# The last 768 tokens' output product by seven half-width products instead of eight

## The chip, the cores and the metric

One core of one Trainium2 chip runs the whole program. The metric is the time of one execution on the device in microseconds (us); the time before is the median of three runs.

## The reference, cut to what matters

```
attention: q, k, v [8 batches, 8 heads, 576, 64]; k and v are averaged over groups of 8 positions (72 left)
  scores = q @ k_pooled.T / 8;  softmax over the 72;  x = attn @ v_pooled     -> x [4608 tokens, 512]
h   = x @ w_in                          # w_in  [512, 2048]
g   = h * clip(h + 3, 0, 6) / 6
out = g @ w_out                         # w_out [2048, 512], out [4608, 512], float32
```

## The kernel before, in words

The 4608 tokens are cut into 12 blocks: 512, 256, 384, 384 and then eight of 384. The first four are plain ("x @ w_in, gate, g @ w_out", lines L822 and L853). The last eight are taken in pairs of 768 tokens, here called supers 0 to 3 (`super_block`). All operands of large products are split into a high and a low part of a 32-bit format that TensorE multiplies at full rate, so each product is three matmuls: high by high, high by low, low by high.

A super has two phases. The **hidden phase** (matmuls at L1065) forms h by a 2x2 split (two token halves of 384, two halves of the 512 inputs, two feature rows of a pair `i`) with seven products instead of eight; its combinations of w_in were formed once, during blocks 2 and 3, and stored in DRAM tiles `wd`. The PSUM sums (`psx`) are copied by ScalarE (`keep`, L1044) or added by VectorE (`plus`, L1039) and gated (L1032, L1033) into `g`. There are 56 products of 6 matmuls with 384 columns each. The **output phase** (matmuls at L1111) is plain: for each of the 16 feature groups f, `split_g` makes the high part (ScalarE, L1050) and the low part (VectorE, L1051) of 128x768 elements of g, and each of six token tiles of 128 takes three matmuls of 512 columns. In super 3 the last token tile is done in two halves of 256 columns, in its own banks, so that its copies start earlier. That makes 288 matmuls in supers 0 to 2 and 240 of 512 plus 96 of 256 columns in super 3.

The weights of both phases stream from DRAM in chunks of 512 KB, one for two products of the hidden phase and one for each f of the output phase. They go through eight SBUF buffers, four in each of two pools (`wsFalse`, `wsTrue`), and `chunk` asks for each one seven ahead. All of these loads, the loads of q, k and v, and the stores of out stand in SyncE's queue (SP), in one order: a transfer that waits holds back those behind it.

The attention of the next two blocks runs within a super: 45% of its steps are spread over the hidden phase and the rest over the output phase (`Paced`). Pooling of k and v is VectorE's (L250, L371), the softmax is ScalarE's and VectorE's with GpSimd dividing (L488). At the end of the output phase `x_ops` forms the seven combinations of x for the next super. Supers 0 to 2 carry such work; super 3 has none, as no block follows.

Within each engine the framework's scheduler sets the order, from its own estimate of times; for the program's first stretch (blocks 0 and 1) a written table (`ORDER`) sets it. The table is the same in both kernels.

Of the kernel before, what the change touches and what calls it, by code (L numbers as in the profile page):

```python
# [17 lines left out]
P = 128  # L18
# [20 lines left out]
RAW = {1: (0, 0), 2: (0, 1), 4: (1, 1)}  # L39
CHUNK, NSTREAM, NFIRST, NC, NREL = 2, 8, 4, 6, 3  # L40
TAIL = 5
# [48 lines left out]
def attention_moe_kernel(  # L90
# [267 lines left out]

    vsum = {}

    def prep_v(b, p):


        if p == 0:
            if b not in W:
                place_v(b)
            sums = ring("vsum")[:, : (NPAIR + NG) * D]
            vsum[b] = sums.rearrange("p (c d) -> p c d", d=D)
        n = P if p < NPAIR else 3 * REM
        vs, st = vsum[b], vraw.pop((b, p))  # L370
        nc.vector.tensor_reduce(  # L371
            out=vs[:n, p], in_=st[:n, : POOL * D].rearrange("p (o d) -> p d o", o=POOL), axis=AX.X, op=ALU.add
        )
        after_mark()
        if p == NPAIR - 1:
            place_heads(b, vs[:, :NPAIR])
        elif p == NPAIR + NG - 1:
            place_rest(b, vs[:, NPAIR:])

    def place_heads(b, vs):  # L380
        whi, wlo, _ = W[b]
        for h in range(2):
            rows, cols = slice(h * D, (h + 1) * D), slice(h * D, (h + 1) * D)
            hi = whi[rows, :, cols]
            nc.scalar.mul(hi, vs[rows], 1.0 / POOL)
# [251 lines left out]
    def side_steps(b):  # L637

        ks = [lambda p=p: load_k(b, p) for p in range(NPAIR)]
        ks += [lambda p=p: prep_k(b, p) for p in range(NPAIR)]  # L640
        vs = []
        n = NPAIR + NG
        for p in range(n + 2):
            if p < n:
                vs.append(lambda p=p: load_v(b, p) if p < NPAIR else load_vr(b, p - NPAIR))
            if p >= 2:
                vs.append(lambda p=p: prep_v(b, p - 2))
        return ks, vs
# [254 lines left out]
    w_dram = [tc.dram_tile([P, CHUNK, 2, 2 * P], F32, name=f"wd{n}") for n in range(len(N1) // CHUNK)]  # L903
    w2_dram = [tc.dram_tile([P, 2, DM], F32, name=f"w2d{f}") for f in range(NF)]

# [27 lines left out]
    def plain_of(i, n):  # L933
        if n < 2:
            for o, (r, q) in list(RAW.items())[2 * n : 2 * n + 2]:
                store(dram_of(i, o), pair_of(i)[r][:, :, q])
        else:
            f = 2 * i + n - 2
            store(w2_dram[f], w_of[f, 1].bitcast(F32))

    late = []
    chunks = [w for _ in supers for w in (*w_dram, *w2_dram)]
    loaded = {}

    def chunk(n, ahead=NSTREAM - 1):

        while (m := len(loaded)) <= n + ahead and m < len(chunks):
            if m % NSTREAM >= NFIRST and len(late) < 2:
                break
            side = m % NSTREAM >= NFIRST  # L950
# [3 lines left out]
            t, src = loaded[m].bitcast(F32), chunks[m]  # L954
            if len(src.shape) == 4:
                src = src.rearrange("p k m c -> p (k m c)")
            else:
                src = src.rearrange("p m c -> p (m c)")
            nc.sync.dma_start(t, src)
            mark()  # L960
        return loaded[n]

    PER = len(w_dram) + len(w2_dram)

    def next_w(n, m):
        t = chunk(n * PER + m // CHUNK)
        return t.rearrange("p (k m c) -> p k m c", k=CHUNK, m=2)[:, m % CHUNK]

    def next_w2(n, f):
        return chunk(n * PER + len(w_dram) + f).rearrange("p (m c) -> p m c", m=2)  # L970

    x_op = {}

    def x_ops(j):
# [3 lines left out]
        def split(o, src):  # L978
            def make(c):
                if c == 0:  # L980
                    x_op[o] = late[0].tile([P, 2, 2, HALF], F32R, name=f"x{o}")
                t, x = x_op[o][:, :, c], src()[:, c]
                nc.scalar.copy(t[:, 0], x)
                nc.vector.tensor_tensor(out=t[:, 1], in0=x, in1=t[:, 0].bitcast(F32), op=ALU.subtract)  # L984

            return [lambda c=c: make(c) for c in range(2)]

# [31 lines left out]
    def super_block(n, j, first_att, second_att):  # L1019

        ops = dict(x_op)
        att_banks[:] = ["a0", "a1", "o3"]
        g_of, chain, parts = {}, {}, {}
        paced = Paced(first_att, len(N1) - 2)
# [17 lines left out]
        def keep(ps):  # L1042
            c = late[1].tile([P, HALF], F32, name="c", bufs=NC)
            nc.scalar.copy(c, ps)  # L1044
            return c

        def split_g(f):
            g = g_of[f // 2][:, f % 2 :: 2]
            hi, lo = (late[1].tile([P, 2, HALF], F32R, name=m, bufs=3) for m in ("ghi2", "glo2"))
            nc.scalar.copy(hi, g)  # L1050
            nc.vector.tensor_tensor(out=lo, in0=g, in1=hi.bitcast(F32), op=ALU.subtract)  # L1051
            mark()
            parts[f] = [t.rearrange("p h t -> p (h t)") for t in (hi, lo)]

        for m, (i, o) in enumerate(N1):
            if o == 1:
                g_of[i] = late[1].tile([P, 4, HALF], F32, name=f"g{i}")
                chain[i] = [bank(["h0", "h1", "o0"], i), bank(["o1"], i), bank(["o2"], i), {}]
# [25 lines left out]
        paced.upto(len(paced.steps))  # L1084

        NT2 = 2 * HALF // P
        rest = x_ops(j + 2) if j + 2 < len(BLOCKS) else []
        paced = Paced(second_att, NT2 * (NF - TAIL))
        split_g(0)
        att_banks[:] = ["a0", "a1"]  # L1090
        banks = ["o0", "h0", "o2", "o1", "h1", "o3"]
        sums = {}
        for f in range(NF):
            if f + 1 < NF:
                split_g(f + 1)
            w = next_w2(n, f)
            for t in range(NT2):
                if f < NF - TAIL:
                    paced.slot()
                elif rest:  # L1100
                    rest.pop(0)()
                hi, lo = (x[:, t * P : (t + 1) * P] for x in parts[f])
                products = (hi, 0), (hi, 1), (lo, 0)
                end = f == NF - 1
                if f == 0:
                    sums[t] = [(slice(0, DM), bank(banks, t, DM))]
                    if n == len(supers) - 1 and t == NT2 - 1:
                        sums[t] = [(slice(0, 256), sums[t][0][1][:, :256]), (slice(256, 512), bank(["a0"], 0, 256))]
                for cols, pos in sums[t]:
                    for k, (l, r) in enumerate(products):  # L1110
                        nc.tensor.matmul(pos, l, w[:, r, cols], start=f == 0 and k == 0, stop=end and k == 2)  # L1111
# [4 lines left out]
                tag, size = ("ro", DM) if t >= 4 else (("ghi2", "glo2")[t % 2], 2 * HALF)  # L1116
                o = late[1].tile([P, size], F32, name="o", tag=tag, bufs=3)[:, :DM]
                at = starts[j] + t * P
                for q, (cols, pos) in enumerate(sums[t]):
                    (nc.vector.tensor_copy if (t + q) % 2 else nc.scalar.copy)(o[:, cols], pos)  # L1120
                    nc.sync.dma_start(out[at : at + P, cols], o[:, cols])
            if f == NF - TAIL - 1:
                paced.upto(len(paced.steps))
        assert not rest

# [281 lines left out]
```

## Time and profile before

| what | value |
|---|---|
| median of 3 runs | 905.71 us (905.52 to 905.98) |
| the profiled execution | 905.32 us, of which the span of instructions is 903.5 us |
| TensorE busy | 884.1 us of 903.5 (98%) |
| VectorE, ScalarE busy | 571.4 us (63%), 513.6 us (57%) |
| DMA | 172.63 MB, mean 191 GB/s |
| granted TensorE clock | 1.00 throughout |

A row of the chain of waits gives the start, the duration and what ran there without a break; a row of the table by stages gives each engine's busy time in a stretch of the span. Busy time of TensorE counts a matmul from its start until its result is modelled to be out, and successive ones overlap: the pace of matmuls is read from their starts, not from their mean durations.

### The profile page before, as it was taken

The numbers are of one execution on the slowest core, as the hardware profiler recorded it, in microseconds if no ns is written. First come the engines' busy times: TensorE is split into PE (matmuls) and PEld (weight loads), VectorE is DVE, ScalarE is ACT, GpSimd is POOL, SyncE is SP. The second block draws the span as 40 slices with busy tenths as digits, with TensorE's granted clock in tenths as the row PEclk, the third lists the DMA queues.
The fourth block names the chain that finished last, engine by engine and source line by source line (L and its number), as shares of the span: only waits on it lengthen the run. The fifth ranks groups of instructions, "written<-read, shape, count | busy, mean of one in ns | idle before, by whom it ended". The sixth has DMA issues, their size and how long they took to land.

```text
span 903.5 us, 14091 instructions
## 1 busy us (share of the span) xinstructions
PE 884.1 (98%) x4760; PEld 796.8 (88%) x4760; DVE 571.4 (63%) x1183; ACT 513.6 (57%) x1473; POOL 86.2 (10%) x168
## 2 busy tenths in 40 slices
PE   7999999999999998999999999999999999999998
PEld 6788888998999987998888999888999888999887
DVE  6999855578876884875735856666677345554221
ACT  5998666656566654765535855454766344444121
POOL 4100002100202010201100100110100110000000
PEclk9999999999999999999999999999999999999999
DMA  9970207984415236977535786744877433767321
GB/s 297 392 278 0 94 1 241 398 293 136 111 52 177 59 129 216 375 251 236 163 104 191 242 281 203 238 154 153 271 249 258 140 117 116 266 231 269 120 70 70
DMA packets 93527, 172.63 MB, mean 191 GB/s; under 512 B 12048, under 2 KB 50704, under 8 KB 93456
## 3 DMA queue, kind: packets, MB, share of 16 engines
q1 hardware_dynamic: 93312, 171.74, 56.9%
q8 instruction: 38, 0.62, 0.3%
q14 instruction: 33, 0.27, 0.1%
q10 hardware_dynamic: 144, 0.00, 0.0%
HBM read 139.20 MB, written 32.51 MB: 190 GB/s over the span
## 4 chain that ended last, share of the span: by engine, by line
PE 83%; DVE 8%; DMA 4%; ACT 2%; SPq 1%; issue 1%; DVEq 0%; ACTq 0%
PE psx L1111 29%; PE psx L1065 25%; PE psh L822 10%; PE pso L853 10%; PE psa L452 3%; PE psa L628 3%; DMA wd<-wq 2%; DMA stage<-q_l 2%; PE psa L558 1%; SPq L928 1%; DVE wq L919 1%; DVE wq L924 1%; DVE wq L926 1%; ACT e L460 1%; DVE x L984 1%
## 5 line engine op out<-in xcount | busy, mean ns | idle before, releaser
L822 PE MATMUL psh<-xhi,w 128*128 128x384 f32 (+2 forms) x520 | 145.4, 339 | 1.1 <-DVE g L834 1.0
L1065 PE MATMUL psx<-x,wsFalse 128*128 128x384 f32 x672 | 130.7, 339 | 2.0 <-ACT o L858 1.0
L1065 PE MATMUL psx<-x,wsTrue 128*128 128x384 f32 x672 | 127.9, 339 | 3.8 <-DVE g L1033 2.6
L1051 DVE TENSOR_TENSOR glo<-g,ghi 128x768 fp32r<-128x768 f32 x64 | 63.5, 993 | 103.9 <-ACT ghi L1050 100.4
L1111 PE MATMUL psx<-wsFalse,ghi 128*128 128x512 f32 (+1 forms) x400 | 123.0, 388 | 0.0
L1111 PE MATMUL psx<-wsTrue,ghi 128*128 128x512 f32 (+1 forms) x400 | 122.7, 386 | 0.0
L853 PE MATMUL pso<-w,ghi 128*128 128x512 f32 x384 | 121.3, 400 | 0.0
L1065 PEld LDWEIGHTS psx<-x,wsTrue 128*128 128x128 f32 x672 | 116.8, 188 | 4.7 <-DVE g L1033 2.9
L1065 PEld LDWEIGHTS psx<-x,wsFalse 128*128 128x128 f32 x672 | 117.2, 188 | 2.9 <-ACT o L858 1.4
L1050 ACT CAST ghi<-g 128x768 fp32r<-128x768 f32 x64 | 53.4, 835 | 95.1 <-PE psx L1111 90.5
L822 PEld LDWEIGHTS psh<-xhi,w 128*128 128x128 f32 x520 | 93.3, 188 | 8.9 <-DVE g L834 1.8
L460 ACT ACTIVATE e<-psa,mx 128x72 f32<-128x72 f32 x256 | 78.3, 322 | 32.4 <-DVE mx L456 31.2
L1039 DVE TENSOR_TENSOR g<-psx,c 128x384 f32<-128x384 f32 x96 | 53.0, 555 | 59.2 <-ACT c L1044 33.3
L488 POOL TENSOR_TENSOR a<-e,sm 128x256 f32<-128x256 f32 x60 | 39.7, 662 | 517.1 <-DVE sm L477 443.0
L822 PE MATMUL psh<-xlo,w 128*128 128x384 f32 (+2 forms) x260 | 86.8, 335 | 0.0
L1111 PEld LDWEIGHTS psx<-wsFalse,ghi 128*128 128x128 f32 x400 | 73.6, 188 | 15.0
L1111 PEld LDWEIGHTS psx<-wsTrue,ghi 128*128 128x128 f32 x400 | 73.4, 188 | 13.4
L853 PEld LDWEIGHTS pso<-w,ghi 128*128 128x128 f32 x384 | 69.1, 188 | 10.2
L1111 PE MATMUL psx<-wsFalse,glo 128*128 128x512 f32 (+1 forms) x200 | 77.6, 388 | 0.0
L1111 PE MATMUL psx<-wsTrue,glo 128*128 128x512 f32 (+1 forms) x200 | 76.6, 383 | 0.0
L853 PE MATMUL pso<-w,glo 128*128 128x512 f32 x192 | 74.0, 399 | 0.0
L1032 ACT ACTIVATE r<-g,small 128x384 f32<-128x384 f32 x96 | 54.7, 612 | 25.5 <-DVE g L1039 21.0
(126 smaller groups left out, 1435.4 us busy)
## 6 DMA issues: line engine op xcount, KB each, us to landing
wsFalse<-wd SPq DMA_DIRECT2D x56, 512.0 KB, 4.5
wsTrue<-wd SPq DMA_DIRECT2D x56, 512.0 KB, 5.0
wsTrue<-w2d SPq DMA_DIRECT2D x32, 512.0 KB, 4.0
wsFalse<-w2d SPq DMA_DIRECT2D x32, 512.0 KB, 3.5
out<-o SPq DMA_DIRECT2D x35, 256.0 KB, 2.7
raw<-w_in_l SPq DMA_DIRECT2D x16, 512.0 KB, 8.5
raw<-w_out_l SPq DMA_DIRECT2D x16, 512.0 KB, 9.3
w2d<-w SPq DMA_DIRECT2D x16, 512.0 KB, 5.4
```

What stands on the lines that cost most here:

```text
L452: nc.tensor.matmul(to, qt[:, p, :], kbds[b % 2][:, p, :], start=r == 0, stop=r == last)
L460: nc.scalar.activation(self.e[:, h], self.ps[:, h], AF.Exp, bias=self.mx[:, h : h + 1], accum_out=self.sm[:, h : h + 1])
L488: engine.tensor_tensor(out=self.a[:, : 4 * D].rearrange("p (h s) -> p h s", h=4), in0=e[:, :, :D], in1=sm[:, :, None].broadcast_to([P, 4, D]),
L628: nc.tensor.matmul(ps, l, r, start=n == 0, stop=n == len(mms) - 1)
L822: nc.tensor.matmul(self.ps, l[f][:, c, :], r[:, c, :], start=c == 0 and i == 0, stop=c == NCC - 1 and i == 2)
L853: nc.tensor.matmul(pos, l, r, start=f == 0 and i == 0, stop=f == NF - 1 and i == 2)
L1032: nc.scalar.activation(r, src, AF.Relu, bias=half_low, scale=GSCALE / (6.0 * WSCALE))
L1039: nc.vector.tensor_tensor(out=g_of[i][:, k], in0=ps, in1=kept, op=ALU.add)
L1050: nc.scalar.copy(hi, g)
L1051: nc.vector.tensor_tensor(out=lo, in0=g, in1=hi.bitcast(F32), op=ALU.subtract)
L1065: nc.tensor.matmul(ps, w[:, l, c * P : (c + 1) * P], t[:, r, c], start=o in (1, 2, 5) and c == 0 and k == 0, stop=c == 1 and k == 2, skip_ ...
L1111: nc.tensor.matmul(pos, l, w[:, r, cols], start=f == 0 and k == 0, stop=end and k == 2)
```

## The change

**Output phase of super 3.** `out_seven` takes the place of the plain phase there. g is split by token half (384) and by feature parity, w_out by parity and by halves of its 512 columns. Seven kinds of products, in the order 1, 2, 4, 5, 6, 7, 3 (`KINDS`), each over four groups `m` of features: 28 steps, each of 3 token tiles x 2 feature rows x 3 matmuls of 256 columns. That is 504 matmuls of 256 columns. Kinds accumulate on each other's PSUM banks where the scheme allows (1, 6 and 7 on `X`; 5 and 3 on `Y`); ScalarE copies the sums of kinds 1, 4, 5 and 6 to SBUF (`to_sbuf`), VectorE adds the other part (`result`) and the store follows. VectorE also forms the combinations of g in place (`mix`), four for each m.

**The blocks of w_out for it.** Kinds 1, 2 and 3 read the stored w_out (`w2d`) in pieces; the other four need combinations. `combine` forms them in the output phases of supers 0 to 2 (three, three and two times), from the chunks that stream by for those phases: six additions and a subtraction on VectorE, one copy on ScalarE, and two stores of 512 KB into new DRAM tiles `w2t`.

**Values.** A pair of value tiles is loaded as two half-pieces and pooled by three wide additions, in place of two strided reductions (L371).

**Smaller things.** Seven stream buffers for eight; tiles for gates, kept sums and split parts in pairs; the combinations of x whole instead of in halves; 50% of the attention steps in the hidden phase instead of 45%; w_out is stored in column halves, so that the plain output phase reads its 512 columns in two pieces of 256.

```diff
-CHUNK, NSTREAM, NFIRST, NC, NREL = 2, 8, 4, 6, 3
+CHUNK, NSTREAM, NFIRST, NC, NREL = 2, 7, 4, 3, 2
+KINDS = (1, 2, 4, 5, 6, 7, 3)
+PLACED = {6: 0, 5: 1, 4: 2, 7: 3}
+RAW2 = {1: (0, 0), 2: (1, 0), 3: (1, 1)}
+SEVEN = (3,)
+MAKE = ((0, 1, 2), (3, 4, 5), (6, 7), ())
+CUTS = (0.5, 0.5, 0.5, 0)
...
     def prep_v(b, p):
-        nc.vector.tensor_reduce(
-            out=vs[:n, p], in_=st[:n, : POOL * D].rearrange("p (o d) -> p d o", o=POOL), axis=AX.X, op=ALU.add
-        )
+        x, y = (vraw.pop((b, p + i))[:n, : POOL * D].rearrange("p (c n) -> p c n", c=2) for i in range(2))
+        for w, a, c in ((4 * D, x, y), (2 * D, x, x[:, :, 2 * D :]), (D, x, x[:, :, D:])):
+            nc.vector.tensor_tensor(out=x[:, :, :w], in0=a[:, :, :w], in1=c[:, :, :w], op=ALU.add)
...
+    def combine(n, i):
+        hi, q = (
+            late[1].tile([P, 2 * DM], F32, name=x, tag="ro", bufs=NREL).rearrange("p (a c) -> p a c", a=4)
+            for x in ("th", "tq")
+        )
+        for r in range(2):
+            w = next_w2(n, 2 * i + r).bitcast(F32)
+            nc.vector.tensor_tensor(out=q[:, 2 * r : 2 * r + 2], in0=w[:, :, 0], in1=w[:, :, 1], op=ALU.add)
+        for to, a, b, how in ((3, 3, 1, ALU.subtract), (1, 1, 0, ALU.subtract), (0, 0, 3, ALU.add), (2, 2, 0, ALU.subtract)):
+            nc.vector.tensor_tensor(out=q[:, to], in0=q[:, a], in1=q[:, b], op=how)
+        nc.scalar.copy(hi.bitcast(F32R), q)
+        nc.vector.tensor_tensor(out=q.bitcast(F32R), in0=q, in1=hi, op=ALU.subtract)
+        for m, x in enumerate((hi, q)):
+            nc.sync.dma_start(w2t_dram[i // 2][:, :, i % 2, m], x)
...
+    def out_plain(n, j, bank, parts, split_g, split_f, pairs, att, rest, last_h):
...
+            if f % 2 == 0 and f // 2 in MAKE[n]:
+                combine(n, f // 2)
...
-                        nc.tensor.matmul(pos, l, w[:, r, cols], start=f == 0 and k == 0, stop=end and k == 2)
+                        to = pos.rearrange("p (q c) -> p q c", c=DM // 2)
+                        nc.tensor.matmul(to, l, w[:, qs, r], start=f == 0 and k == 0, stop=end and k == 2)
...
+    def out_seven(n, j, bank, parts, split_g, split_f, pairs, att, rest, last_h):
+        todo = [(o, m) for o in KINDS for m in range(NM)]
+        sets = {"X": ["o2", "o1"], "Z": ["o0", "o3"], "V": ["h1", "h0"], "Y": ["o0", "o3"]}
+        on = {2: "Z", 1: "X", 4: "V", 5: "Y", 6: "X", 7: "X", 3: "Y"}
...
+        for x, (o, m) in enumerate(todo):
+            upto(x + 2)
+            w, t = next_w2(n, x), parts[o, m]
+            for i in range(NT2):
+                to = ps[name][i // 2][:, i % 2 * W2 : (i % 2 + 1) * W2]
+                for k in range(2):
+                    for y, (l, r) in enumerate(((0, 0), (0, 1), (1, 0))):
+                        nc.tensor.matmul(
+                            to,
+                            t[:, l, k, i * P : (i + 1) * P],
+                            w[:, k, r],
...
+                        )
+            if m < NM - 1:
+                continue
+            if o in (1, 4, 5, 6):
+                to_sbuf(o)
+            if o == 2:
+                result(1, 0, 0, "Z")
+            elif o == 7:
+                result(5, 1, 1, "X")
+                result(4, 1, 0, "X")
+            elif o == 3:
+                result(6, 0, 1, "Y")
```

**How instructions move.** Three places follow. In a row stand the line, the operation, what it writes and reads, its size and how often it is repeated; numbers in names tell tiles of one kind apart.

VectorE, at the turn from the hidden to the output phase of super 3 (`g` are the gated sums, `glo` and `part` the low parts for the output phase), before:

```order
L1039 TENSOR_TENSOR g_9012<-psx,c 128x384 x2
L1033 SCALAR_TENSOR_TENSOR g_9012<-r,g_9012 128x384 x2
L1033 SCALAR_TENSOR_TENSOR g_9012<-r,psx 128x384
L1051 TENSOR_TENSOR glo_9172<-g_8568,ghi_9171 128x768
L1051 TENSOR_TENSOR glo_9199<-g_8641,ghi_9198 128x768
L1051 TENSOR_TENSOR glo_9226<-g_8641,ghi_9225 128x768
```

and now:

```order
L1080 TENSOR_TENSOR g_8840<-psx,c 128x384 x2
L1074 SCALAR_TENSOR_TENSOR g_8840<-r,g_8840 128x384 x2
L1074 SCALAR_TENSOR_TENSOR g_8840<-r,psx 128x384
L1094 TENSOR_TENSOR part<-g_8840,part 128x768
L1196 TENSOR_TENSOR g_8840<-g_8840 128x2x384
L1094 TENSOR_TENSOR part<-g_8440,part 128x768
L1196 TENSOR_TENSOR g_8840<-g_8840 128x2x384
L1094 TENSOR_TENSOR part<-g_8560,part 128x768
L1094 TENSOR_TENSOR part<-g_8700,part 128x768
```

The splits go on as before; two of the combinations of g (L1196) stand between them here, and six of the first eight have moved up into the hidden phase.

VectorE, at the end of super 2's output phase (`x`, `mid` and the numbered `x` are the next super's combinations, `o` the copies for the stores), before:

```order
L1051 TENSOR_TENSOR glo_8453<-g_7745,ghi_8452 128x768
L992 TENSOR_TENSOR mid<-x 128x768
L984 TENSOR_TENSOR x_8409<-x,x_8409 128x384
L992 TENSOR_TENSOR x<-x 128x768
L984 TENSOR_TENSOR x_8426<-mid,x_8426 128x384 x2
L992 TENSOR_TENSOR x<-x,mid 128x768
L984 TENSOR_TENSOR x_8383<-x,x_8383 128x384 x2
L992 TENSOR_TENSOR x<-x 128x768
L984 TENSOR_TENSOR x_8398<-x,x_8398 128x384 x2
L984 TENSOR_TENSOR x_8441<-x,x_8441 128x384 x2
L1120 COPY o<-psx 128x512 x3
```

and now:

```order
L1094 TENSOR_TENSOR part<-g_7613,part 128x768
L1000 TENSOR_TENSOR tq<-wsTrue 128x512 x2
L1029 TENSOR_TENSOR x<-x 128x768
L1021 TENSOR_TENSOR x_8319<-x,x_8319 128x768
L1003 TENSOR_TENSOR tq<-tq 128x256
L1021 TENSOR_TENSOR x_8341<-x,x_8341 128x768
L1003 TENSOR_TENSOR tq<-tq 128x256 x2
L1177 COPY o<-psx 128x512
L1003 TENSOR_TENSOR tq<-tq 128x256
L1177 COPY o<-psx 128x512
L1006 TENSOR_TENSOR tq<-tq,th 128x1024
L1177 COPY o<-psx 128x512
```

The last combination of w_out (`tq`, `th`) stands among the last copies that free PSUM banks for super 3.

SyncE's queue at the same place, before:

```order
L959 DMA wsFalse<-wd_97 128x1024
L959 DMA wsFalse<-wd_98 128x1024
L1121 DMA out<-o 128x512 x5
L959 DMA wsFalse<-wd_99 128x1024
L1121 DMA out<-o 128x512
L959 DMA wsTrue<-wd_100 128x1024
```

and now:

```order
L977 DMA wsTrue<-wd_97 128x1024
L1178 DMA out<-o 128x512 x4
L1009 DMA w2t_127<-th 512x1x256
L1178 DMA out<-o 128x512
L977 DMA wsTrue<-wd_98 128x1024
L1009 DMA w2t_127<-tq 512x1x256
L1178 DMA out<-o 128x512
L977 DMA wsTrue<-wd_99 128x1024
```

Two stores of `w2t` have come between the stores of out, and the seventh and eighth weight chunks of super 3 (`wd_98`, `wd_99`) stand behind them.

More of the change, by code (lines that the diff above doesn't have):

```diff
@@ L642, in side_steps @@
         n = NPAIR + NG
[L643 to L647, printed above, removed]
+        for p in range(n):
+            vs.append(lambda p=p: load_v(b, p))
+            if p and (p % 2 == 0 or p == n - 1):
+                vs.append(lambda p=p: prep_v(b, (p - 1) // 2 * 2))
         return ks, vs
@@ L903, in attention_moe_kernel @@
     w_dram = [tc.dram_tile([P, CHUNK, 2, 2 * P], F32, name=f"wd{n}") for n in range(len(N1) // CHUNK)]
[L904 removed]
+    w2_dram = [tc.dram_tile([P, 4, 2, 2, DM // 2], F32, name=f"w2d{m}") for m in range(NF // 4)]
+    w2t_dram = [tc.dram_tile([P, len(PLACED), 2, 2, DM // 2], F32, name=f"w2t{m}") for m in range(NF // 4)]
     def dram_of(i, o):
@@ L938, in plain_of, with chunks_of @@
             f = 2 * i + n - 2
-            store(w2_dram[f], w_of[f, 1].bitcast(F32))
+            for m in range(2):
+                w = w_of[f, 1][:, m].bitcast(F32).rearrange("p (q c) -> p q c", q=2)
+                store(w2_dram[f // 4][:, f % 4, :, m], w)
     late = []
-    chunks = [w for _ in supers for w in (*w_dram, *w2_dram)]
+    def chunks_of(n):
+        if n not in SEVEN:
+            plain = [w2_dram[f // 4][:, f % 4].rearrange("p q m c -> p (q m c)") for f in range(NF)]
+        else:
+            plain = []
+            for o in KINDS:
+                for m in range(NF // 4):
+                    if o in RAW2:
+                        r, q = RAW2[o]
+                        plain.append(w2_dram[m][:, r::2, q].rearrange("p k m c -> p k (m c)"))
+                    else:
+                        plain.append(w2t_dram[m][:, PLACED[o]].rearrange("p k m c -> p (k m c)"))
+        return [w.rearrange("p k m c -> p (k m c)") for w in w_dram] + plain
+    chunks, first_of = [], []
     loaded = {}
@@ L978, in split, with make @@
         def split(o, src):
[L979 to L986, printed above, removed]
+            def make():
+                t = x_op[o] = late[0].tile([P, 2, 2, HALF], F32R, name=f"x{o}")
+                nc.scalar.copy(t[:, 0], src())
+                nc.vector.tensor_tensor(out=t[:, 1], in0=src(), in1=t[:, 0].bitcast(F32), op=ALU.subtract)
+            return [make]
         mid = []
@@ L1022, in super_block @@
         att_banks[:] = ["a0", "a1", "o3"]
-        g_of, chain, parts = {}, {}, {}
+        g_of, pairs, chain, parts = {}, {}, {}, {}
+        r_of, c_of = [], []
         paced = Paced(first_att, len(N1) - 2)
@@ L1084, in super_block @@
         paced.upto(len(paced.steps))
+        rest = x_ops(j + 2) if j + 2 < len(BLOCKS) else []
+        att_banks[:] = ["a0", "a1"]
+        (out_seven if n in SEVEN else out_plain)(n, j, bank, parts, split_g, split_f, pairs, second_att, rest, last_h)
+        assert not rest
+    def out_plain(n, j, bank, parts, split_g, split_f, pairs, att, rest, last_h):
         NT2 = 2 * HALF // P
[L1087 to L1090, printed above, removed]
+        paced = Paced(att, NT2 * (NF - TAIL))
+        split_f(0)
         banks = ["o0", "h0", "o2", "o1", "h1", "o3"]
-        sums = {}
+        sums, outs = {}, []
         for f in range(NF):
             if f + 1 < NF:
-                split_g(f + 1)
+                split_f(f + 1)
             w = next_w2(n, f)
+            if f % 2 == 0 and f // 2 in MAKE[n]:
+                combine(n, f // 2)
             for t in range(NT2):
@@ L1101, in super_block @@
                     rest.pop(0)()
-                hi, lo = (x[:, t * P : (t + 1) * P] for x in parts[f])
+                hi, lo = (parts[f][:, m].rearrange("p h t -> p (h t)")[:, t * P : (t + 1) * P] for m in range(2))
                 products = (hi, 0), (hi, 1), (lo, 0)
@@ L1115, in super_block @@
                     continue
-                tag, size = ("ro", DM) if t >= 4 else (("ghi2", "glo2")[t % 2], 2 * HALF)
-                o = late[1].tile([P, size], F32, name="o", tag=tag, bufs=3)[:, :DM]
+                if t % 3 == 0:
+                    o3 = late[1].tile([P, 4 * HALF], F32, name="o", tag="part", bufs=3)
+                o = o3[:, t % 3 * DM : (t % 3 + 1) * DM]
                 at = starts[j] + t * P
-                for q, (cols, pos) in enumerate(sums[t]):
-                    (nc.vector.tensor_copy if (t + q) % 2 else nc.scalar.copy)(o[:, cols], pos)
+                for x, (qs, pos) in enumerate(sums[t]):
+                    cols = slice(qs.start * 256, qs.stop * 256)
+                    (nc.vector.tensor_copy if (t + x) % 2 else nc.scalar.copy)(o[:, cols], pos)
                     nc.sync.dma_start(out[at : at + P, cols], o[:, cols])
```

154 lines of the change are left out of this document (106 added, 48 removed).

## The prediction

> **What bounds the kernel now.** I read the page's busy times first, then the stages of the super blocks (a super's hidden phase, then its output phase, from 347 us on), then TensorE's waits.
>
> ```profile
> PE 884.1 (98%) x4760; PEld 796.8 (88%) x4760; DVE 571.4 (63%) x1183; ACT 513.6 (57%) x1473; POOL 86.2 (10%) x168
> ...
> 347.00:416.00 69.00, 64.61 (x378) 63.76 (x379) 50.20 (x107) 48.09 (x142) 6.04 (x13) 1.00 0.89 304
> 416.00:491.50 75.50, 75.50 (x368) 62.94 (x367) 40.92 (x74) 31.39 (x90) 6.83 (x12) 1.00 0.47 153
> ...
> 699.60:773.50 73.90, 73.90 (x345) 61.25 (x344) 33.09 (x63) 30.98 (x92) 7.33 (x12) 1.00 0.39 129
> 773.50:833.00 59.50, 58.85 (x338) 58.53 (x337) 31.04 (x59) 29.18 (x58) 0.00 (x0) 1.00 0.77 263
> 833.00:899.70 66.70, 66.70 (x336) 56.29 (x335) 14.69 (x17) 13.19 (x17) 0.00 (x0) 1.00 0.25 84
> 899.70:903.50 3.80, 0.03 (x1) 0.00 (x0) 0.14 (x1) 0.37 (x1) 0.00 (x0) 1.00 0.66 236
> ```
>
> Columns after the stretch and its length: TensorE, its weight loads, VectorE, ScalarE, GpSimd (busy, instructions), granted clock, DMA share, GB/s. TensorE fills every output phase: 75.50 of 75.50, 73.90 of 73.90, 66.70 of 66.70. VectorE has about half of these phases free. So time falls where TensorE's work falls, and nowhere else unless something new makes it wait. Its present waits in the supers are few:
>
> ```profile
> PE psx L1065 <- DVE g L1033: 2.6, 1, 2.6
> PE psx L1065 <- DVE g L1039: 2.1, 3, 0.9
> PE psx L1065 <- ACT o L858: 1.0, 1, 1.0
> ```
>
> That is 5.7 us, all in hidden phases.
>
> **The pace of matmuls** decides. From the chain of waits (start, duration, what, how many) and from the output phase of super 3 in order of time, where 256 and 512 columns stand side by side:
>
> ```profile
> 143.78 1.40 PE pso L853 x6
> 145.18 1.40 PE psh L822 x12
> ...
> 168.93 0.98 PE psa L452 x8
> ...
> 773.54 57.48 PE psx L1065 x330
> ...
> 832.98 66.76 PE psx L1111 x336
> ```
> ```profile
> 870.43 0.62 PE L1111 MATMUL psx<-wsFalse,ghi 128*128 128x512 f32 x2
> ...
> 873.93 0.39 PE L1111 MATMUL psx<-wsFalse,ghi 128*128 128x256 f32 x2
> ...
> 874.63 0.62 PE L1111 MATMUL psx<-wsFalse,ghi 128*128 128x512 f32 x2
> ```
>
> Fifteen matmuls of 512 columns take 873.93 - 870.43 = 3.50 us, 233 ns each; six of 256 take 0.70 us, 117 ns each; 384 columns take 57.48/330 = 174 ns. In block 1, twelve of 256 in a row take as long as six of 512: 1.40 us. So the pace is in proportion to the columns, with a fixed part of a few ns at most. The floor under it is the weight load before each matmul: the eight score matmuls of 144 columns come at 0.98/8 = 122 ns, not at the 66 ns of their columns, and 117 ns lies at that floor or just above it. Twelve in a row is the longest stretch seen; 504 are asked for. I take 118 ns, with 117 and 122 as ends.
>
> **The change part by part.**
>
> 1. *Output phase of super 3.* Removed: 240 matmuls of 512 and 96 of 256 columns, 66.76 us by the chain. Added: 504 of 256 columns: 504 x 0.118 = 59.5 us (59.0 to 61.5). Difference -7.3 us (-7.8 to -5.3). It is seven eighths of the columns: 66.76 x 7/8 = 58.4 agrees.
>
> 2. *Waits within that phase.* Kind 7 follows kind 6 on the same banks (`X`), so TensorE waits for ScalarE to copy kind 6's sums.
>
> ```profile
> L1120 ACT COPY o<-psx 128x512 f32<-128x512 f32 x12 | 7.0, 587 | 17.8 <-PE psx L1111 17.8
> L1050 ACT CAST ghi<-g 128x768 fp32r<-128x768 f32 x64 | 53.4, 835 | 95.1 <-PE psx L1111 90.5 <-DVE g L1033 4.3
> L1051 DVE TENSOR_TENSOR glo<-g,ghi 128x768 fp32r<-128x768 f32 x64 | 63.5, 993 | 103.9 <-ACT ghi L1050 100.4 <-PE psx L1111 3.4
> L1039 DVE TENSOR_TENSOR g<-psx,c 128x384 f32<-128x384 f32 x96 | 53.0, 555 | 59.2 <-ACT c L1044 33.3 <-PE psx L1065 25.7
> ```
>
> The first bank is complete six matmuls (0.7 us) before kind 6 ends, and its copy of 512 columns takes 0.59: I take 0.3 us for what remains with the hand-over, 0 to 1.4 (both copies behind the end). Splits: a step lasts 18 x 0.118 = 2.1 us, and with three buffers a split may begin when the step three before its own is over, which leaves two steps (4.2 us) to make 0.84 + 0.99 us. Behind it on VectorE stand the additions of results (by the 555 ns for 384, about 0.7 for 512 and 0.45 for 256 columns) and combinations of g (0.95). The worst place is the end of kind 7: four additions, 2.3 us, then a split, 3.3 in all, against 4.2. Hidden, by 0.9 us; if the slack is gone, under 1 us a place. At the start, three splits and six of the eight first combinations are already made in the hidden phase, where VectorE is busy 31.04 of 59.50 us.
>
> 3. *The stream.* 28 loads of 512 KB in 60 us replace 16 in 67; this is the hidden phase's rate (28 in 59.5 us), which runs there at 263 GB/s without a wait.
>
> ```profile
> wsFalse<-wd SPq DMA_DIRECT2D x56, 512.0 KB, 4.5
> wsTrue<-wd SPq DMA_DIRECT2D x56, 512.0 KB, 5.0
> raw<-w_out_l SPq DMA_DIRECT2D x16, 512.0 KB, 9.3
> ```
>
> With seven buffers a load is asked for six steps ahead, 6 x 2.1 = 12.6 us, against 5.0 us to land (9.3 at the slowest of this size). Nothing, 0 to 2.6 us (the longest wait of TensorE in the supers).
>
> 4. *The end.* Before, seven stores follow in the last 7 us; now four leave two microseconds after kind 7, over 6 us before the end, and two at the end.
>
> ```profile
> 896.94 4.07 SPq L1121 DMA_DIRECT2D out<-o  x7
> ```
>
> The last six matmuls run beside the first addition; then 0.45 us of addition in place of the last copy of 0.37, but one store behind fewer others (SyncE spaces them by 0.5 us). I take -0.2 (-0.6 to +0.4) of the 3.80 us.
>
> 5. *Combinations of w_out*, eight in the output phases of supers 0 to 2:
>
> ```profile
> L919 DVE TENSOR_TENSOR wq<-w 128x256 f32<-128x256 f32 x32 | 12.5, 430 | 13.0 <-DMA wd<-wq 12.9
> L926 DVE TENSOR_TENSOR wq<-wq 128x512 fp32r<-128x512 f32 x16 | 11.3, 706 | 3.6 <-ACT wq L925 3.3
> L924 DVE TENSOR_TENSOR wq<-wq 128x128 f32<-128x128 f32 x64 | 19.4, 303 | 1.0
> ...
> L371 DVE TENSOR_REDUCE vsum<-vst x36: 1035/1065/1087, 170.2 to 692.4; 128x64 f32<-128x512 f32 x24, 96x64 f32<-96x512 f32 x12
> ```
>
> Two additions of 512 (0.71), four of 256 (0.43) and a subtraction of 1024 (about 1.3, by 993 ns for 768): 4.4 us each, 35 us of VectorE in all; a copy of 1024 on ScalarE, about 1.1 us each, 9 us. Values give back: 36 reductions of 1.065 us (the last row: least, median, most) become 18 triples of 0.71 + 0.43 + 0.30 = 1.44 us, 38 against 26: -12 us. Per output phase of super 0 that is 40.92 + 13 - 2 = 52 of 75.5 us on VectorE. The cover is TensorE's own 67 to 75 us; here a step is 18 matmuls of 233 ns, 4.2 us, and a split has two of them, 8.4 us, longer than one combination and the split itself (4.4 + 1.8). At the end of super 2's phase the last combination stands among three copies that free banks; from the last split on VectorE has 1.4 + 3 x 0.95 + 4 x 0.43 + 3 x 0.7 + 1.3 = 9.4 us, and that split can begin three steps (12.6 us) before the phase ends and be done 10.8 us before. It just fits; the bank copied last (`o3`) isn't used by super 3's hidden phase. Its `w2t` stores hold the two tiles that the next gates write (`ro`), and stand ahead of chunks seven and eight; those are wanted 12 us later. I take +0.4 us for all of this, -2 to +4: below, if the shorter pooling or the moved attention take a third of the 5.7 us of waits away; above, if half of the eight combinations make TensorE wait 1 us.
>
> 6. *Two pieces of 256 for 512 columns* in supers 0 to 2: 864 matmuls. No row has this; pairs of 64 columns in the opening stretch are as fast as whole rows within 5 ns (below), so 0, up to 864 x 5 ns = 4.3 us.
>
> ```profile
> L329 PE MATMUL psa<-stage,ident 128*128 128x128 f32 x32 | 3.8, 278 | 2.0 <-DMA stage<-v_l 2.0
> L547 PE MATMUL psa<-ident,stage 128*128 128x128 f32 x16 | 2.4, 273 | 0.0
> ```
>
> 7. *Moved attention (45% to 50%), the halves of x joined, pairs of tiles, w_out stored in halves:* TensorE's work is the same; joined halves save fixed parts (two of 552 ns become 993). Counted in item 5.
>
> Sum: -7.3 + 0.3 + 0 - 0.2 + 0.4 + 0 = -6.8 us. The profiled execution took 905.32 us, 0.39 under the median of 905.71; on the median's scale that is **898.9 us**. No change can be told within about 0.2%, 1.8 us.
>
> **The rivals.**
>
> *A. Late VectorE in the output phases (the other side).* Each combination is 4.4 us in one queue, ahead of attention's maxima and low parts, for which TensorE waits in order. If each of the eight delays TensorE by 2 us, 16 us are lost: 905.7 - 7.2 + 16 = 914.5. It ends above the time before once a combination costs over 0.9 us. For it: hidden phases, with VectorE 73% busy (50.20 of 69.00), are where the present waits are. Against it: after the change the output phase stands at 69% in super 0, and at under 60% in super 2.
>
> *B. A fixed cost per matmul.* With a fixed part in each matmul, 504 short ones cost more than the 336 before. At 133 ns each the phase takes 67 us and nothing is won: 905.7; that would be a fixed part of 33 of the 233 ns. The rows above (117 for 256, 174 for 384, 233 for 512 columns) leave a few ns; that no stretch longer than twelve was seen is all that speaks for it. The Trainium skill (TensorE: Matmul & The Clock Gate, section Back-to-back issue gap) gives sustained paces of 81 ns for 128 and 131 ns for 512 columns where each matmul has its weight load. By a straight line between these, an estimate, 256 columns would cost 98 ns, and the phase would lose 504 x 98 - (240 x 131 + 96 x 98) ns = 8.5 us, for about 914. The trace disagrees with that ratio of three quarters: it has one half.
>
> *C. The stream falls behind.* Seven buffers, and loads queued behind `w2t` stores: one wait of 2.6 us as now in super 0, in the last phase too: 901.5, and twice that, 904. For it: in super 0's hidden phase the DMA share is 0.89. Against it: 0.77 in super 3's, without a wait.
>
> *D. Split reading is slower* (item 6): 898.9 + 4.3 = 903.2.
>
> **How the numbers follow.** Forecast 0.75, A 0.09, B 0.04, C 0.06, D 0.06. The forecast's own range is 896 to 902 (the ends of items 1 to 5, not all at once). Leaving A and B out and taking in C and D to 903.5 leaves under 2 in 10 outside: 896.0 to 903.5. Faster by over 0.2%: the forecast, C, and D but for its edge: 0.84. Slower: A mostly, 0.09. The rest, 0.07, is B and the mild forms of A.
>
> **What would show it.** In the new profile: 504 matmuls of 256 columns in the last output phase, starts 118 ns apart and the phase 59 to 60 us long; TensorE without an idle row there but at most 0.3 us where kind 7 begins; a tail of about 3.6 us; the output phases of supers 0 to 2 still near 75, 74 and 74 us (with somewhat less attention in them) and their matmuls of 512 at 233 ns; no wait of TensorE for `part`, `tq` or weight chunks. I am wrong if starts lie 125 ns apart or more, if the three earlier supers together grow by over 3 us, or if a wait above 1 us shows in the last phase.

## The result, and the profile after

The changed kernel takes 899.72 us in the median (897.50 to 901.72, six runs), against 905.85 us for the kernel before on the same chip: a ratio of 0.9935 (95% interval 0.9922 to 0.9949), or 6 us less. The forecast was 898.9, within 896.0 to 903.5. The profiled execution took 898.7 us, with a span of 896.9.

The busy times on the page of the changed kernel, and its stages (columns as in the prediction: TensorE, weight loads, VectorE, ScalarE, GpSimd, clock, DMA share, GB/s):

```profile
PE 878.7 (98%) x4928; PEld 799.6 (89%) x4928; DVE 620.4 (69%) x1274; ACT 533.1 (59%) x1481; POOL 87.0 (10%) x168
```
```profile
341.50:415.90 74.40, 72.37 (x422) 70.47 (x421) 54.28 (x122) 51.56 (x155) 7.24 (x14) 1.00 0.83 275
415.90:489.90 74.00, 74.00 (x354) 61.43 (x353) 47.30 (x89) 31.76 (x78) 6.45 (x10) 1.00 0.62 201
...
700.80:773.60 72.80, 72.80 (x337) 60.27 (x336) 38.48 (x66) 29.50 (x73) 6.20 (x10) 1.00 0.47 150
773.60:833.00 59.40, 58.83 (x337) 58.49 (x336) 37.36 (x65) 30.46 (x59) 0.00 (x0) 1.00 0.84 273
833.00:893.30 60.30, 60.30 (x506) 59.98 (x504) 37.01 (x45) 24.91 (x35) 0.00 (x0) 1.00 0.69 225
```

VectorE does 49 us more work than before, and TensorE does not notice: the output phases of supers 0 and 2 are still filled to the last hundredth (74.00 of 74.00, 72.80 of 72.80). The last output phase begins at 833.0, as before (833.0 in the prediction's rows), and is now 60.3 us long where it was 66.7. Its tail is 896.9 - 893.3 = 3.6 us, where it was 3.8. So 6.4 + 0.2 = 6.6 us, and 905.32 - 6.6 is the 898.7 of this execution: all of the gain stands in the last phase.

The chain that ended last (start, duration, what, how many), and TensorE's waits in the supers:

```profile
773.78 56.53 PE psx L1113 x324
...
833.21 59.44 PE psx L1239 x498
892.64 0.02 issue
892.67 0.69 DVE kept L1219
893.36 0.02 issue
893.38 0.42 DVE kept L1219
```
```profile
PE psa L456 <- DMA qt<-q_l: 1.4, 2, 0.7
PE psx L1113 <- ACT c L1088: 1.2, 2, 0.6
PE psx L1113 <- DVE g L1080: 0.7, 1, 0.7
PE psx L1113 <- DMA wsTrue<-wd: 0.7, 1, 0.7
```

498 of the 504 short matmuls stand in the chain as one piece of 59.44 us, 119.4 ns each. The waits listed sum to 4.0 us; before they were 5.7 by the prediction's list, 6.2 with one of 0.5 us for `vrem` that it leaves out. Those for `g` have shrunk from 2.6 and 2.1 to 0.7, while new ones for the queries (`qt`, 1.4), for `c` (1.2) and for a weight chunk (`wd`, 0.7) have come. None stands in the last phase.

### The profile page after: what moved, and what is told of

It is laid out like the page before. It is cut to its first block, busy times and chain, and to the rows that moved or that the text cites. A ratio compares the mean times of both kernels' runs of the same rounds, so it can differ in the third digit from the quotient of the medians.

```text
span 896.9 us, 14551 instructions
## 1 busy us (share of the span) xinstructions
PE 878.7 (98%) x4928; PEld 799.6 (89%) x4928; DVE 620.4 (69%) x1274; ACT 533.1 (59%) x1481; POOL 87.0 (10%) x168
## 4 chain that ended last, share of the span: by engine, by line
PE 90%; DMA 5%; DVE 3%; ACT 1%; issue 1%; SPq 0%; DVEq 0%; ACTq 0%
PE psx L1113 25%; PE psx L1166 22%; PE pso L856 14%; PE psh L825 14%; PE psx L1239 7%; PE psa L456 4%; PE psa L632 4%; PE psa L562 1%; DMA raw<-w_in_l 1%; DMA raw<-w_out_l 1%; DMA wd<-wq 1%; DMA qt<-q_l 1%; ACT e L464 1%; DMA wsTrue<-wd 1%; DMA stage<-k_l 1%
## 5 line engine op out<-in xcount | busy, mean ns | idle before, releaser
L1113 PE MATMUL psx<-x,wsFalse 128*128 128x384 f32 x768 | 148.8, 339 | 0.6 <-ACT c L1088 0.6
L1166 PE MATMUL psx<-wsFalse,part 128*128 128x512 f32 x504 | 124.2, 398 | 0.0
L1094 DVE TENSOR_TENSOR part<-g,part 128x768 fp32r<-128x768 f32 x76 | 74.2, 976 | 64.4 <-ACT part L1093 63.6
L1166 PEld LDWEIGHTS psx<-wsFalse,part 128*128 128x128 f32 x504 | 93.3, 188 | 20.3
L1093 ACT CAST part<-g 128x768 fp32r<-128x768 f32 x76 | 63.6, 836 | 75.7 <-PE psx L1166 47.5
L1113 PEld LDWEIGHTS psx<-x,wsTrue 128*128 128x128 f32 x576 | 100.1, 188 | 2.7 <-DVE g L1080 1.8
L1166 PE MATMUL psx<-wsTrue,part 128*128 128x512 f32 x360 | 86.3, 393 | 0.0
L1166 PEld LDWEIGHTS psx<-wsTrue,part 128*128 128x128 f32 x360 | 66.6, 188 | 13.3
L1074 DVE SCALAR_TENSOR_TENSOR g<-r,g 128x384 f32<-128x384 f32 x96 | 53.9, 570 | 17.0 <-ACT r L1073 16.7
L1088 ACT COPY c<-psx 128x384 f32<-128x384 f32 x96 | 44.1, 481 | 23.2 <-PE psx L1113 22.6
```

The source lines that it names most:

```text
L1074: nc.vector.scalar_tensor_tensor(out=g_of[i][:, k], in0=r, scalar=GSCALE, in1=src, op0=ALU.min, op1=ALU.mult)
L1093: nc.scalar.copy(t[:, 0], src)
L1094: nc.vector.tensor_tensor(out=t[:, 1], in0=src, in1=t[:, 0].bitcast(F32), op=ALU.subtract)
L1113: nc.tensor.matmul(ps, w[:, l, c * P : (c + 1) * P], t[:, r, c], start=o in (1, 2, 5) and c == 0 and k == 0, stop=c == 1 and k == 2, skip_ ...
L1166: nc.tensor.matmul(to, l, w[:, qs, r], start=f == 0 and k == 0, stop=end and k == 2)
```

## The experiments

Each version was timed together with the kernel before, so versions are compared by their ratios to it.

**1. The change without the seven products.** The stream, the shorter pooling, the moved attention and the joined halves stay; w_out isn't combined and the last super is computed by the plain products.

```
-SEVEN = (3,)
-MAKE = ((0, 1, 2), (3, 4, 5), (6, 7), ())
+SEVEN = ()
+MAKE = ((), (), (), ())
```

> The changed kernel with the plain output phase in super 3 as well and no combinations of w_out; pooling by wide additions, seven buffers, pairs of tiles, moved attention and column halves all stay. Theory 1 (the whole gain is the matmul pace of the last output phase, 66.8 against 60.0 us, and the rest of the change comes to nothing): 906 us, between 904.5 and 907.5, not told from the kernel before. Theory 2 (the rest wins some 2 us by pooling and the smaller things, and the combinations of w_out eat it): 903.5 to 904, faster than before by 0.2%.

Measured: 906.68 against 905.49 us, ratio 1.0020 (1.0006 to 1.0033). Its chain has the old length again, and one of its waits has grown:

```profile
834.12 66.81 PE psx L1166 x336
```
```profile
PE psx L1113 <- DMA wsTrue<-wd: 2.3, 2, 1.2
```

So the rest of the change gains nothing: it costs 0.5 to 3.0 us. The gain is the seven products' alone.

**2. The same with w_out combined but not used.** The combinations are made and stored; the last super is plain.

```
-SEVEN = (3,)
+SEVEN = ()
```

> The same with the eight combinations of w_out and their stores left in; their results are not used. Theory 1 (VectorE has room for them beside TensorE): within 1 us of the run without them, about 906. Theory 2: slower than that by 2 us or more, the difference lying in the output phases of supers 0 to 2.

Measured: 907.60 against 905.49, ratio 1.0027 (1.0017 to 1.0037). The combinations are the difference to experiment 1, 0.9 us, which these intervals don't separate from nothing. From here to the changed kernel only the last phase's products change: 1.0027 to 0.9935 is 0.92%, 8.3 us by the two ratios, 7.5 us by the two profiled spans (904.4 and 896.9). Of these 7.5, the last phase and its tail give 6.8; 0.7 stand before them, and there experiment 2's execution has 3.4 us at half the granted clock (near 14 us), which the changed kernel's has not.

**3. The pooling of values as before** (one reduction per tile, one load per tile), with the rest of the change.

```
-        for w, a, c in ((4 * D, x, y), (2 * D, x, x[:, :, 2 * D :]), (D, x, x[:, :, D:])):
-            nc.vector.tensor_tensor(out=x[:, :, :w], in0=a[:, :, :w], in1=c[:, :, :w], op=ALU.add)
+            sums = ring("vsum")[:, : (NPAIR + NG) * D]
+            vsum[b] = sums.rearrange("p (c d) -> p c d", d=D)
...
```

> The changed kernel with the values pooled by the two strided reductions of before (and loaded and placed as before). Theory 1 (12 us of VectorE's time are saved beside TensorE and are worth nothing): within 1 us of the changed kernel, 899 to 901 us. Theory 2 (the pooling is what pays for the combinations of w_out): 2 us or more slower than the changed kernel, about 902 us. If it is faster, the new pooling itself costs: the idle of TensorE near 191 and 217 us in the changed kernel, 2.5 us, would then be gone, 897.5.

Measured: 900.67 against 905.20, ratio 0.9949 (0.9932 to 0.9966): not told apart from the changed kernel's 0.9935. So the times show no worth of the 12 us of VectorE that the wide additions give back; by the intervals it is at most some 3 us.

**4. Attention at 45% again.**

```
-CUTS = (0.5, 0.5, 0.5, 0)
+CUTS = (0.45, 0.45, 0.45, 0)
```

> The changed kernel with 45% of the attention steps in the hidden phase, as before, in place of 50%. Theory 1 (TensorE's work is the same): within 1 us of the changed kernel. Theory 2 (the moved steps bring the waits for q at 411 us, 1.4 us in super 0's hidden phase): about 1.3 us faster, 898.4.

Measured: 899.06 against 905.20, ratio 0.9936 (0.9918 to 0.9954), the same as the changed kernel. The waits for `qt` have gone, but a wait of 0.9 us for attention's sums has come and those for `c` have grown from 1.2 to 2.1 us.

**5. Fewer buffers in the kernel before.** The seven buffers were the term costed at nothing. Three versions of the kernel before, all else unchanged (`NSTREAM` counts the buffers, `NFIRST` splits them between the two kinds):

```
-CHUNK, NSTREAM, NFIRST, NC, NREL = 2, 8, 4, 6, 3
+CHUNK, NSTREAM, NFIRST, NC, NREL = 2, 7, 4, 6, 3
```

> The kernel before with seven stream buffers instead of eight and nothing else changed. Theory 1 (a load is asked for 12 us ahead and lands in 5): 905.5, not told from before. Theory 2 (the smaller stream is what makes the rest of the change 1 to 2 us slower, as the run with the plain last phase was): 906.5 to 907.5.

Measured: 908.39 against 905.20, ratio 1.0035 (1.0021 to 1.0049).

```
+CHUNK, NSTREAM, NFIRST, NC, NREL = 2, 7, 3, 6, 3
```

> The kernel before with seven stream buffers, three in the first pool and four in the second, where the run before had four and three. Theory S: the same cost, about 908. Theory O (the cost comes with one particular order): anything between 904 and 909, with TensorE's waits at other places than 405 to 418 us.

Measured: 910.71 against 905.94, ratio 1.0055 (1.0038 to 1.0072).

```
+CHUNK, NSTREAM, NFIRST, NC, NREL = 2, 6, 3, 6, 3
```

> The kernel before with six stream buffers, three in each pool. Theory S (the stream's depth is what cost 0.35% with seven: loads land too late): the cost grows clearly, to 910 us or more, with TensorE waiting for weight chunks. Theory O (fewer buffers only move the loads in SyncE's queue and with them the attention's order; the depth is enough): no growth, 905 to 909 us, and hardly a wait for chunks.

Measured: 910.01 against 905.94, ratio 1.0047 (1.0030 to 1.0064).

The hidden phase of super 0 in the kernel before, then with seven (4 and 3), seven (3 and 4) and six buffers, one row from each profile:

```profile
340.40:415.80 75.40, 70.84 (x409) 68.91 (x409) 52.54 (x114) 48.68 (x143) 5.84 (x13) 1.00 0.83 283
```
```profile
341.70:418.40 76.70, 70.92 (x410) 68.80 (x409) 53.94 (x114) 49.39 (x143) 7.26 (x14) 1.00 0.81 272
```
```profile
341.20:421.10 79.90, 74.02 (x410) 71.64 (x409) 53.08 (x114) 49.32 (x144) 5.95 (x14) 0.96 0.78 267
```
```profile
339.90:418.50 78.60, 72.52 (x410) 70.30 (x409) 53.72 (x115) 49.70 (x144) 6.77 (x14) 0.98 0.78 265
```

The stage lasts 75.4, 76.7, 79.9 and 78.6 us. TensorE's longest wait in it is for a weight chunk in all three, which it isn't in the kernel before:

```profile
PE psx L1065 <- DMA wsTrue<-wd: 2.2, 1, 2.2
```
```profile
PE psx L1065 <- DMA wsTrue<-wd: 3.3, 1, 3.3
```
```profile
PE psx L1065 <- DMA wsTrue<-wd: 3.4, 1, 3.4
```

The kernel before also waits near 355 us, for 2.6 us (`g`). So the waits for chunks are longer only by 0.7 and 0.8 us in the last two, and 0.4 shorter in the first. The larger part of what the last two lose in this stage is TensorE's busy time, which grows from 70.84 to 74.02 and 72.52 us: after the wait they run at half clock for a while (last section). For 3 and 4 buffers this stage explains 4.5 of the 6.4 us between the profiled executions, and for six 3.2 of 2.6. For 4 and 3 it explains 1.3 of 4.4 us; 1.3 come before it and 1.7 between it and the last phase, and what causes them is not shown. (The profiled executions with seven buffers were the slowest of six each, that with six the fastest of seven.) So with three buffers in the first pool the price lies mainly in the stage with the highest DMA share; with 4 and 3, the split of the changed kernel, that is not shown. In none does it lie in the last phase. Six are no worse than seven (3 and 4), so the number of buffers alone doesn't set the price; which order of instructions comes with it was not taken apart. The changed kernel with eight buffers wasn't tried.

**6. Seven products for two supers.**

```
-SEVEN = (3,)
-MAKE = ((0, 1, 2), (3, 4, 5), (6, 7), ())
+SEVEN = (2, 3)
+MAKE = ((0, 1, 2, 3), (4, 5, 6, 7), (), ())
```

> Seven half-width products in the output phases of supers 2 and 3; the combinations of w_out are made four each in supers 0 and 1. Theory 1: super 2's output phase gives its 6.7 us as super 3's did: 893 us, 892 to 895. Theory 2 (super 2's phase also holds attention and the next super's combinations of x, so VectorE, 33 us before, gets 15 us of combinations of g and 12 us of further splits in a phase of 67 us, and TensorE waits for it): at most half of that, 896 us or more.

Measured: 897.44 against 905.49, ratio 0.9915 (0.9898 to 0.9931): 0.2% below the changed kernel, with intervals that overlap, where a second full gain would be 0.7%. In super 2's output phase, up to where super 3's hidden phase begins to mix with it (763 us), the short matmuls keep TensorE filled:

```profile
704.00:764.00 60.00, 59.68 (x491) 59.48 (x490) 45.33 (x70) 36.75 (x87) 8.69 (x12) 1.00 0.73 236
```

From the start of super 2's output phase to the end of super 3's hidden phase it takes 831.7 - 704.1 = 127.6 us, the changed kernel 833.0 - 700.8 = 132.2: 4.6 us less, of which the earlier stages give back 3.3. In super 0's hidden phase it is 1.8 us (76.2 against 74.4):

```profile
341.90:418.10 76.20, 73.88 (x421) 71.94 (x420) 54.70 (x125) 51.94 (x155) 7.39 (x15) 0.98 0.82 269
```

**7. Two supers, attention at 45%,** to see whether the waits for `qt` in experiment 6 (2.0 us in three) were what was given back.

```
-SEVEN = (3,)
-MAKE = ((0, 1, 2), (3, 4, 5), (6, 7), ())
-CUTS = (0.5, 0.5, 0.5, 0)
+SEVEN = (2, 3)
+MAKE = ((0, 1, 2, 3), (4, 5, 6, 7), (), ())
+CUTS = (0.45, 0.45, 0.45, 0)
```

> Seven half-width products in supers 2 and 3 as in the run before, with 45% of the attention in the hidden phase. If the 2.8 us of waits in super 0's hidden phase (for q, at 411 to 414 us) come from the moved steps, they go and the time is about 895.5; if they come from the order that the scheduler happens to find, 896.5 to 898.5, with waits elsewhere.

Measured: 896.88 against 905.20, ratio 0.9911 (0.9890 to 0.9931). The waits for `qt` fell to 0.7 us, others rose (2.1 us for `c`, 1.4 for a weight chunk), and the time can't be told from experiment 6.

**8. Three supers,** all eight combinations in super 0's output phase.

```
-SEVEN = (3,)
-MAKE = ((0, 1, 2), (3, 4, 5), (6, 7), ())
+SEVEN = (1, 2, 3)
+MAKE = ((0, 1, 2, 3, 4, 5, 6, 7), (), (), ())
```

> Seven half-width products in supers 1, 2 and 3; all eight combinations of w_out in super 0. Theory 1 by TensorE's work alone: three times 6.7 us, 886 us. Theory 2: eight combinations of 4.4 us bring VectorE in super 0's output phase to 41 + 35 - 2 = 74 of 75 us, so that TensorE waits there by several us: 890 to 900 us, and the waits stand in super 0's output phase.

Measured: 898.73 against 905.49, ratio 0.9928 (0.9912 to 0.9944): no better than one super. Its stages, super 0's output phase, and super 1's output phase with the mixed turn into super 2's hidden phase:

```profile
414.30:488.40 74.10, 74.10 (x355) 61.49 (x355) 60.52 (x115) 35.19 (x82) 6.44 (x10) 1.00 0.73 238
558.00:639.00 81.00, 75.06 (x584) 74.18 (x583) 61.71 (x106) 47.10 (x127) 11.07 (x13) 0.96 0.77 250
```
```profile
PE psa L562 <- POOL a L492: 3.1, 1, 3.1
PE psa L456 <- DMA qt<-q_l: 1.5, 1, 1.5
```

The first row is the strongest test of rival A: all eight combinations in one phase, VectorE 60.52 of 74.10 us busy, and TensorE doesn't lose a hundredth. What fails is the second: TensorE idles 6 of 81 us, 4.6 of it in these two waits, both for attention; 0.9 more is a wait for a low part (`part`), which is rival A's mechanism in small. After the wait of 3.1 us the clock is at half for 6.8 us (last section). That attention is late because the output phase beside it is shorter is argued, not shown.

**9. Three supers with attention moved later,** to take these waits away.

```
-CUTS = (0.5, 0.5, 0.5, 0)
+CUTS = (0.45, 0.6, 0.55, 0)
```

> Seven half-width products in supers 1, 2 and 3 as before, with the attention's share in the hidden phase at 45, 60 and 55% in supers 0, 1 and 2 in place of 50%. The run with 50% lost some 7 us to waits of TensorE for divided scores and q in super 1's output phase, where VectorE had work for 52 of 70 us. If the attention that stood there is the cause, those waits fall to under 3 us and the time to 893 to 895; if VectorE's additional work is, they stay and move to the hidden phase, 897 to 900.

Measured: 903.35 against 905.94, ratio 0.9964 (0.9949 to 0.9979): 0.36% worse than experiment 8, and slower than both expectations. In the profiled execution, the slowest of twelve, super 1's hidden phase, 67.0 us in the changed kernel, lasts 88.0. It holds more of the attention (60% for 50%), TensorE waits in it, and behind the waits of 2.0 and 4.1 us its clock is at half for 10.2 and 6.8 us (the whole phase, then the first of these stretches):

```profile
491.00:579.00 88.00, 77.89 (x421) 75.53 (x422) 64.45 (x131) 57.16 (x181) 12.71 (x22) 0.90 0.72 235
504.00:514.20 10.20, 8.77 (x27) 8.25 (x28) 6.01 (x12) 6.58 (x27) 3.86 (x6) 0.50 0.35 115
```
```profile
PE psa L456 <- DMA qt<-q_l: 5.6, 2, 4.1
PE psa L456 <- ACT e L464: 2.0, 1, 2.0
```

**10. Two supers, 45%, and the kinds in another order,** so that the two kinds on the same banks don't follow each other.

```
-KINDS = (1, 2, 4, 5, 6, 7, 3)
+KINDS = (1, 2, 4, 6, 5, 7, 3)
```

> Seven half-width products in supers 2 and 3 with 45% of the attention in the hidden phase, kind 6 done before kind 5, so that another kind stands between 6 and 7 on the same banks. The wait at kind 7's start, 0.23 us in the changed kernel, goes from both phases: 896.4 against 896.9, which the times can't tell; in the trace no gap at that place.

Measured: 896.24 against 905.94, ratio 0.9901 (0.9882 to 0.9920), the best of all versions: 0.8 to 1.2% under the kernel before; its interval and the changed kernel's just fail to overlap, while it can't be told from experiments 6 and 7. The order's own part is small, as the last piece of its chain shows:

```profile
834.18 59.24 PE psx L1239 x498
```

59.24 for 59.44 us: the 0.2 us of the changed kernel's hand-over.

## Why the prediction was right, by its steps

*Item 1, the pace:* 118 ns taken, 119.4 measured over 498 in a row (the hand-over of item 2 included); the phase became shorter by 6.4 to 6.6 us with item 2, where 7.0 were forecast. The weight loads take longer than the pace, as the changed kernel's row for the last phase's line shows (least, median, most ns), but they overlap:

```profile
L1239 PEld LDWEIGHTS psx<-wsFalse,part x288: 187/188/193, 834.4 to 888.6; 128*128 128x128 f32 x144
```

That is rival B refuted: twelve in a row were enough to forecast 498. The prediction's reading of 122 ns as the floor of a weight load was not right: in the trace of the kernel before, starts of matmuls of 192 columns (L628) lie 111 ns apart and those of transposes of 128 columns (L558) 108; what does set the floor is not shown. By a straight line, an estimate, the Trainium skill's figures (TensorE: Matmul & The Clock Gate, section Back-to-back issue gap) made 256 columns cost three quarters of 512; the measured 119 and 233 ns make it one half.

*Item 2, the hand-over:* 0.3 us taken. Where kind 7 begins (875.7 us) two starts are 240 and 223 ns apart where the others are 119, 0.23 us in all.

*Item 3, the stream:* costed at nothing, argued from the last phase. There it held. But the seven buffers serve the whole kernel, and the kernel before loses 3.2 us by them alone (experiment 5). If a term was mis-sized, it is this one: the prediction read it in the one stage that the change rewrites, and rival C too put its wait into the last phase, though it named super 0's DMA share of 0.89. In the whole change little of it shows: the changed kernel's hidden phase of super 0 has 74.4 us where it had 75.4. One of the prediction's signs did fail, though: it expected no wait for weight chunks, and one of 0.7 us stands in super 2's hidden phase. What seven buffers cost within the changed kernel was not measured.

*Item 4, the tail:* -0.2 taken, 3.80 to 3.60 measured.

*Item 5, combinations and pooling:* the costs on their engines were right. In the changed kernel (VectorE's groups, then ScalarE's):

```profile
L1003 DVE TENSOR_TENSOR tq<-tq 128x256 f32<-128x256 f32 x32 | 13.8, 430 | 0.6
L1006 DVE TENSOR_TENSOR tq<-tq,th 128x1024 fp32r<-128x1024 f32 x8 | 9.8, 1223 | 3.4 <-ACT th L1005 3.4
L377 DVE TENSOR_TENSOR vst<-vst 128x512 f32<-128x512 f32 x12 | 8.7, 726 | 1.0 <-DMA vst<-v_l 1.0
L1000 DVE TENSOR_TENSOR tq<-wsFalse 128x512 f32<-128x512 f32 x9 | 6.0, 704 | 1.2 <-DMA w2t<-th 1.2
L377 DVE TENSOR_TENSOR vst<-vst 128x256 f32<-128x256 f32 x12 | 5.0, 418 | 0.2
L377 DVE TENSOR_TENSOR vst<-vst 128x128 f32<-128x128 f32 x12 | 3.4, 284 | 0.1
```
```profile
L1005 ACT CAST th<-tq 128x1024 fp32r<-128x1024 f32 x8 | 8.4, 1051 | 7.6 <-DVE tq L1003 7.6
```

One combination is 2 x 0.70 + 4 x 0.43 + 1.22 = 4.3 us (4.4 forecast), its copy 1.05 (1.1), a triple of the pooling 0.73 + 0.42 + 0.28 = 1.43 (1.44). As a delay, items 3 and 5 together were +0.4; experiment 1 and 2 give +1.8 (0.5 to 3.0) and +2.4 us (1.5 to 3.4), within item 5's range of -2 to +4. Of that only the 0.9 us between the two is the combinations', and that isn't told from nothing.

*Item 6, split reading:* nothing taken. In super 2's output phase 74 matmuls in two pieces of 256 columns take 17.05 us, 230 ns each, where whole rows took 233. Rival D falls. (The rows that the prediction compared were durations, not distances between starts; these are.)

*The rivals:* A did not happen in the change, nor in super 0's output phase with all the combinations in it; one wait of its kind, 0.9 us, stands in experiment 8. C did not happen in the last phase; its mechanism, a wait for a weight chunk, showed in super 0 of the kernel before with fewer buffers (experiment 5), in versions 0.35 to 0.55% slower.

The sum held to 0.8 us. Items 1, 2 and 4 gave 6.6 us in the profiled execution where 7.2 were forecast. The medians gained 6.1 us (4.6 to 7.1 by the ratio's interval), which leaves -0.5 to 2.0 us for items 3 and 5 together, where 0.4 was forecast; the profiled execution shows none (the last phase begins at 833.0 in both), and experiment 1's 1.8 us was measured with a plain last phase. So the last phase was forecast by its mechanism, while that the small terms came out so near is in part luck: the runs don't know them to better than 2 us.

## What to carry to other kernels

When an engine is full, price fewer columns by the measured distance between starts of the two shapes and take the gain only for the stage that runs them; here 119 against 233 ns held from twelve to 498. Price a smaller ring of buffers in every stage that streams through it, the one with the highest DMA share first, and not only where the change uses it. And the same trick applied again is not worth the same again: by the ratios the second super gave a third to a half as much and the third nothing. In their traces new waits for attention and loads, and a half clock behind some of them, stand in the place of the work removed; that these are all of the reason is not shown.

## What was not expected of the hardware

A wait of TensorE can cost more than its length. In the kernel before with seven buffers (3 and 4), the 3.3 us without a chunk are followed by a stretch at half the granted clock; the same with six buffers:

```profile
352.20:355.10 2.90, 0.33 (x2) 0.01 (x1) 1.27 (x3) 1.55 (x3) 0.00 (x0) 1.00 1.02 318
355.10:361.90 6.80, 6.02 (x19) 6.05 (x20) 2.45 (x4) 0.82 (x2) 0.00 (x0) 0.50 1.03 392
361.90:365.00 3.10, 3.10 (x20) 3.10 (x19) 0.73 (x2) 2.06 (x4) 0.00 (x0) 0.99 1.03 396
```
```profile
354.60:358.00 3.40, 2.95 (x9) 2.98 (x10) 0.66 (x2) 0.06 (x1) 0.00 (x0) 0.50 1.06 386
```

19 matmuls take 6.02 us (317 ns each) in the second row. By the trace their starts lie 320 ns apart there and 174 again in the third, whose count includes two that began before it. At 174 ns the 19 would take 3.3, so the wait costs 2.7 us more after it is over, which with 1.4 us of longer waits is 4.1 of the 4.5 that this stage grew by.

Experiments 8 and 9 show the same: after a wait of 3.1 us the clock is half for 6.8 us, and after one of 4.1 for 6.8. All four waits of 3.1 us and more were followed by it. Of the shorter ones, those of the kernel before (2.6 and 2.0 us) and of seven buffers (4 and 3; 2.2) weren't; experiment 10 (2.4, half for 3.4 us) and experiments 1, 2 and 7 near 11 us (2.5, 2.3 and 1.9, each 3.4 us) were, and so was experiment 9's wait of 2.0 us, which follows others of 1.1 and 0.6 within 7 us (10.2 us at half). In experiment 6 two waits for `qt` within 2.6 us sufficed; half of the 3.4 us behind them, 1.7 us by estimate, is most of the 1.8 us that its super 0 lost. So between 1.9 and 2.6 us the length of a wait alone does not decide in these runs. The Trainium skill (TensorE: Matmul & The Clock Gate, section What's actually happening) gives an idle window of about 3.4 us for the fall to half and as long a busy one for the return; stretches of 3.4, 6.8 and 10.2 us agree, the falls after waits of 1.9 to 2.5 us don't agree with an idle time of that length.

It is also in the spread of the times. Of 51 executions of the kernel before, the 23 with a mean clock of 0.999 or more took 904.3 us in the mean, the 28 below it 906.4, and each of the three groups that were timed together shows the same (1.8 to 2.6 us). These 2.1 us, 0.2%, are a third of what the change gained. In which stage the clock fell in those executions is not recorded, and that it caused the difference is not shown.
